# An instruction order from list schedules made forwards and backwards, in a fused attention and two-layer network kernel

## The chip, the cores and the metric

The kernel runs on one core of a Trainium2 chip. The metric is the device time of one execution in microseconds (us); lower is better. Of several runs the median counts.

## The reference

Attention over q, k, v of shape 4 x 8 x 576 x 64 (batch, heads, sequence, head size), in float32, with a mask that lets a block of 64 queries see its own and all earlier blocks of 64 keys. Its output, reshaped to 2304 tokens of 512 numbers, goes through two networks:

```python
x = attention(q, k, v)                               # softmax(q k^T / 8 + block mask) v
h = np.maximum(np.maximum(x @ w1, x @ w2), x @ w3)   # w1, w2, w3: 512 x 768
y = h @ w_out                                        # 768 x 512
h = y @ w_in                                         # 512 x 2048 (moe2)
out = (h * np.cos(h)) @ w_out2                       # 2048 x 512
```

## The kernel before

Matmuls of the networks run in a float32 form of which TensorE takes one pass, so every operand is split into a high and a low part and each product is three matmuls (high x high, high x low, low x high). The weights arrive as 64-bit numbers; `convert` makes a high and a low float32 matrix out of each piece of 128 x 512: two scalings, a shift, an and-or, an add, a copy to the high part and a subtraction for the low part. Three of these (and-or, add, subtraction) and the shift always run on VectorE (DVE); the copies and scalings may go to ScalarE (ACT) or VectorE.

**Attention** is 32 items: a batch, one half of the sequence (320 or 256 queries) and a pair of heads. For each item: the scores S (one PSUM buffer, `S`), the row maximum by a VectorE reduction (`stat`), the exponential by ScalarE into the single buffer `prob`, a division by the row sums, transposes on TensorE (`tb`, copied to `pt`), the product with v (`X`) and the split of the result into `xhi` and `xlo`. The first 8 items use plain float32 matmuls, the others the split form.

**The first network** (`moe1_units`) can start on a half of a batch when its four items are done; its three weight pieces per column tile (`whi`, `wlo`) and the output weights (`vhi`, `vlo`) have to be converted by then. Its results (`y`) go to DRAM. **The second network** (`hstage`, `ostage`) runs in chunks of 512 tokens, the last of 256: for each of 16 column tiles `hstage` does 12 matmuls into `psm`, VectorE and ScalarE form h cos(h) and split it (`gh`, `gl`), and `ostage` adds 12 matmuls into the `po` banks two tiles later. Its weights and inputs lie in four pools: `w_in` tiles 0 to 6 and the inputs of the even chunks in `wb`, the other `w_in` tiles in `wc`, the inputs of the odd chunks in `wk2`.

None of this is issued as it is written. The program records operations in a `Plan`: each has its engine, an estimated cost, the operations that it depends on, and its place in the program (`order`). `run` then does a list schedule: it keeps a clock for each engine, takes the engine that can start next, and gives it, of the operations that are ready at that time, the one that comes first in the program. For operations with several possible engines (`ways`) it picks one by estimated end. Each operation is issued the moment it is scheduled, so that this order is the order in each engine's instruction stream. A buffer of a rotation (`bufs` places under one `tag`) may be used once all operations on the buffer `bufs` generations older are done (`older`); which of the places it gets is left to the pool, which hands them out in the order in which buffers are first used. Because every operation is issued through one line of `caller`, line 209, nearly all rows of the profile carry that line, and groups are told apart by their tiles.

Of the kernel before, what the change touches and what calls it, by code (L numbers as in the profile page):

```python
# [101 lines left out]
class Pool:  # L102
# [1 line left out]
        self.plan, self.kw, self.real, self.open_op, self.bufs, self.tags = plan, kw, None, None, [], {}  # L104

    def tile(self, shape, dt, name, tag=None, bufs=1):
        older = None
        if tag is not None:
            gens = self.tags.setdefault(tag, [])
            older = gens[-bufs] if len(gens) >= bufs else None  # L110
        tag = tag or name
        buf = Buf(self, shape, lambda: self.real.tile(shape, dt, name=name, tag=tag, bufs=bufs),
                  self.kw.get("space") == PSUM, dt, older)
        self.bufs.append(buf)
        self.tags.setdefault(tag, []).append(buf)
        dims, step = [], 1
        for n in reversed(shape[1:]):
            dims.insert(0, (0, n, step))
            step *= n
        return View(buf, dims, (), shape[0])  # L120
# [10 lines left out]
class Plan:  # L131
# [20 lines left out]
    def open(self, *after, **kw):  # L152
        pool = Pool(self, kw)
        o = pool.open_op = self.op("CTL")
        o.deps |= {p.close_op for p in after}

        def run():
            pool.real = self.tc.alloc_tile_pool(**kw)
        o.calls.append(run)
        return pool  # L160
# [114 lines left out]
        return (n * 3.3 + 75 if method == "tensor_tensor" else max(400.0, n * 1.04 + 195)), 45.0, method != "memset"  # L275


    def run(self):
        for o in self.ops:
            if o.engine == "CTL":  # L280
                if hasattr(o, "pool"):
                    for b in o.pool.bufs:
                        o.deps |= set(b.ops)
                continue
            for b in o.bufs:
                o.deps.add(b.pool.open_op)
                if b.older is not None:
                    o.deps |= set(b.older.ops)
            o.deps.discard(o)
        users = {o: [] for o in self.ops}  # L290
        missing = {o: len(o.deps) for o in self.ops}
        for o in self.ops:
            for d in o.deps:
                users[d].append(o)
        free = dict.fromkeys(("PE", "DVE", "ACT", "POOL", "SP"), 0.0)
        ready = {e: [] for e in free}
        waiting = {e: [] for e in free}
        load = dict.fromkeys(free, 0.0)
        end, issued, bus, port = {}, 0, 0.0, 0.0

        def finish(o, start, stop):
            end[o] = (start, stop)
            for fn in o.calls:
                fn()
            for u in users[o]:
                missing[u] -= 1
                if not missing[u]:
                    release(u)

        def release(o):  # L310
            at = 0.0
            for d in o.deps:
                if d.engine == "PE" and o.engine == "PE":
                    at = max(at, end[d][1] - d.late)
                else:
                    at = max(at, end[d][1] + (0.0 if d.engine == "CTL" or o.engine == "CTL" else
                                              self.CROSS if end[d][1] > self.EARLY else 35.0))
            if o.engine == "CTL":
                nonlocal issued
                issued += 1  # L320
                finish(o, at, at)
            else:
                if o.ways:
                    def done(way):
                        e, (cost, late, shared), _ = way
                        start = max(free[e] + load[e], at)
                        if shared:
                            start = max(start, port)
                        return start + cost * self.WEIGHT[e] + late
                    o.engine, (o.cost, o.late, o.port), call = min(o.ways, key=done)  # L330
                    o.calls = [call]
                load[o.engine] += o.cost
                heapq.heappush(waiting[o.engine], (at, o.order, o))

        for o in self.ops:
            if not missing[o] and o not in end and not o.deps:
                release(o)
        while issued < len(self.ops):
            best = None
            for e in free:  # L340
                while waiting[e] and waiting[e][0][0] <= free[e]:
                    at, order, o = heapq.heappop(waiting[e])
                    heapq.heappush(ready[e], (order, at, o))
                if ready[e]:
                    t, pick = free[e], ready[e][0]
                    if pick[2].port and port > t:
                        others = [x for x in ready[e] if not x[2].port]
                        if others:
                            pick = min(others)
                        else:  # L350
                            t = port
                elif waiting[e]:
                    pick = waiting[e][0]
                    t = max(pick[0], port if pick[2].port else 0.0)
                else:
                    continue
                if best is None or t < best[0]:
                    best = (t, e, pick)
            assert best, "the plan has a cycle"
            t, e, pick = best  # L360
            o = pick[2]
            if ready[e]:
                ready[e].remove(pick)
                heapq.heapify(ready[e])
            else:
                heapq.heappop(waiting[e])
            cost = o.cost * (2 if e == "PE" and t < self.COLD else 1)
            free[e] = t + cost
            load[e] -= o.cost
            stop = t + cost + o.late  # L370
            if o.port:
                port = t + cost
            if e == "SP":
                bus = max(bus, t + o.cost) + (o.late - 2000.0)
                stop = bus + 2000.0
            issued += 1
            finish(o, t, stop)
        self.length = max(s[1] for s in end.values())
        self.end = end


def fused_kernel(tc, qk, v2, w1, w2, w3, wout, w_in2, w_out2, out):
# [558 lines left out]
```

## Time and profile before

| | us |
|---|---|
| median of 3 runs | 941.53 |
| lowest and highest run | 940.58 and 943.83 |
| span of the profiled execution, first to last instruction | 944.3 |

Of the profiled execution only the span is given; it lies 2.8 us above the median of the runs and 0.5 us above the highest. The engines in the profile are PE (TensorE's matmuls), PEld (its weight loads), DVE (VectorE), ACT (ScalarE), POOL (GpSimd) and SP (SyncE, which issues the transfers).

### The profile page before, as it was taken

Reading aid. Unit: us, or ns where it says so; the run is one execution under the profiler, and the core shown is the slowest. Engines: PE = TensorE matmul, PEld = TensorE weight load, DVE = VectorE, ACT = ScalarE, POOL = GpSimd, SP = SyncE. Lnnn points to the kernel's source line nnn. Section 1 sums busy time; section 2 is a strip of 40 time slices with the busy share of each in tenths; the row PEclk is TensorE's granted clock in tenths of the full one; section 3 lists DMA queues with packets and bytes.
Section 4 is the critical chain, followed back from the end, with each engine's and each line's share of the span. In section 5 each row is a group of like instructions: output and inputs, shape, how many; then the busy total and the mean of one; then the engine's idle time right before and its main releaser. Section 6 shows DMA issues by size and latency. Waiting matters only on the chain.

```text
span 944.3 us, 14297 instructions
## 1 busy us (share of the span) xinstructions
PE 910.2 (96%) x5388; PEld 806.1 (85%) x5388; DVE 660.9 (70%) x1394; ACT 483.0 (51%) x1088; POOL 0.7 (0%) x7
## 2 busy tenths in 40 slices
PE   5888999999999999999999999999999999999998
PEld 4656989989999999999999988888888888888897
DVE  7878868789888877677676988854555455545454
ACT  5857467677767666656564663332224223322233
POOL 0000000000000000000000000000000000000000
PEclk7989999999999999999999999999999999999999
DMA  6544342433344411212003593120001000100010
GB/s 205 157 153 154 120 140 77 166 111 112 127 143 128 135 51 47 68 41 87 15 1 115 162 386 103 45 66 24 1 1 67 1 1 1 45 0 1 1 45 23
DMA packets 39492, 78.51 MB, mean 83 GB/s; under 512 B 9728, under 2 KB 20992, under 8 KB 39424
## 3 DMA queue, kind: packets, MB, share of 16 engines
q1 hardware_dynamic: 39424, 77.61, 25.4%
q8 instruction: 42, 0.69, 0.3%
q14 instruction: 26, 0.21, 0.1%
HBM read 61.34 MB, written 16.25 MB: 82 GB/s over the span
## 4 chain that ended last, share of the span: by engine, by line
PE 79%; DVE 10%; ACT 7%; issue 2%; DMA 1%; SPq 0%; ACTq 0%
PE psm L209 45%; PE po L209 21%; PE S L209 7%; ACT prob L209 5%; PE tb L209 4%; DVE stat L209 3%; PE X L209 2%; DVE t L209 1%; DVE x L209 1%; DVE vs L209 1%; DVE pt L209 1%; DMA vr<-v 1%; DVE hm L209 1%; ACT pt L209 0%; DMA qk<-qk 0%
## 5 line engine op out<-in xcount | busy, mean ns | idle before, releaser
L209 PE MATMUL psm<-yh,w_in 128*128 128x512 f32 (+1 forms) x640 | 195.8, 372 | 0.0
L209 PE MATMUL psm<-xhi,whi 128*128 128x320 f32 (+1 forms) x576 | 176.6, 307 | 2.9 <-DVE hm L209 1.3
L209 PE MATMUL po<-w_out,gh 128*128 128x512 f32 x576 | 178.8, 392 | 0.0
L209 PE MATMUL psm<-xlo,whi 128*128 128x320 f32 (+1 forms) x576 | 170.9, 297 | 1.2 <-DVE xlo L209 1.2
L209 PE MATMUL psm<-xhi,wlo 128*128 128x320 f32 (+1 forms) x576 | 170.9, 297 | 0.0
L209 ACT ACTIVATE th<-th,halfpi 128x512 f32<-128x512 f32 (+1 forms) x80 | 54.5, 681 | 185.4 <-DVE th L209 185.3
L209 PEld LDWEIGHTS psm<-yh,w_in 128*128 128x128 f32 x640 | 117.2, 188 | 22.8 <-DVE th L209 0.4
L209 PEld LDWEIGHTS po<-w_out,gh 128*128 128x128 f32 x576 | 107.0, 188 | 23.2 <-ACT gh L209 0.4
L209 PE MATMUL psm<-yl,w_in 128*128 128x512 f32 (+1 forms) x320 | 118.8, 371 | 0.0
L209 PEld LDWEIGHTS psm<-xhi,whi 128*128 128x128 f32 x576 | 109.7, 190 | 5.9 <-DVE hm L209 2.8
L209 PE MATMUL po<-w_out,gl 128*128 128x512 f32 x288 | 112.5, 391 | 0.0
L209 PEld LDWEIGHTS psm<-xlo,whi 128*128 128x128 f32 x576 | 109.6, 190 | 1.5 <-DVE xlo L209 1.4
L209 PEld LDWEIGHTS psm<-xhi,wlo 128*128 128x128 f32 x576 | 109.4, 190 | 0.0
L209 DVE TENSOR_SCALAR th<-psm 128x512 int32<-128x512 f32 (+1 forms) x80 | 50.9, 637 | 73.8 <-PE psm L209 70.5
L209 ACT ACTIVATE prob<-S,stat 128x320 f32<-128x320 f32 (+8 forms) x144 | 74.7, 526 | 47.1 <-DVE stat L209 43.3
L209 DVE TENSOR_REDUCE stat<-S 128x1 f32<-128x320 f32 (+8 forms) x144 | 64.5, 485 | 46.6 <-PE S L209 35.5
L209 DVE TENSOR_TENSOR th<-psm,th 128x512 f32<-128x512 f32 (+1 forms) x80 | 51.0, 637 | 53.9 <-ACT th L209 53.9
L209 DVE TENSOR_TENSOR gl<-th,gh 128x512 fp32r<-128x512 f32 (+1 forms) x80 | 50.9, 636 | 37.6 <-ACT gh L209 37.4
L209 ACT CAST gh<-th 128x512 fp32r<-128x512 f32 (+1 forms) x76 | 43.7, 575 | 53.8 <-DVE th L209 53.8
L209 PEld LDWEIGHTS psm<-yl,w_in 128*128 128x128 f32 x320 | 60.2, 188 | 11.5
L209 PE MATMUL tb<-ident,prob 128*128 128x128 f32 x400 | 60.9, 284 | 5.6 <-DVE pt L209 3.2
L209 PEld LDWEIGHTS po<-w_out,gl 128*128 128x128 f32 x288 | 54.1, 188 | 11.7 <-DVE gl L209 0.2
(86 smaller groups left out, 1523.4 us busy)
## 6 DMA issues: line engine op xcount, KB each, us to landing
raw<-w SPq DMA_DIRECT2D x18, 512.0 KB, 3.6
raw<-w_in SPq DMA_DIRECT2D x16, 512.0 KB, 3.8
raw<-w_out SPq DMA_DIRECT2D x16, 512.0 KB, 3.8
vr<-v SPq DMA_DIRECT2D x16, 320.0 KB, 3.4
qk<-qk SPq DMA_DIRECT2D x12, 416.0 KB, 3.5
kept_in<-both SPq DMA_DIRECT2D x9, 512.0 KB, 2.8
w_in<-kept_in SPq DMA_DIRECT2D x9, 512.0 KB, 10.2
out<-osb SPq DMA_DIRECT2D x18, 256.0 KB, 2.0
```

What stands on the lines that cost most here:

```text
L209: return lambda: getattr(real, method)(*[value(a) for a in args], **{k: value(a) for k, a in kw.items()})
```

## The change

`run` no longer issues operations while it schedules. It calls `forward` and `backward` in turn, 8 times. `forward` is the list schedule of before, except that among the ready operations of an engine it takes the one with the lowest `rank`; in the first pass the rank is the place in the program. `backward` makes a list schedule from the end of the program to its start, on the engines that the forward pass chose, and notes for each operation the time at which it starts there, counted from the beginning, with the length of the forward pass as the end. That time is the rank of the next forward pass. Of the 8 forward passes the one with the shortest planned length is issued, in its order and with its choice of engines. Costs, dependencies and the rule that an engine never idles while one of its operations is ready stay as they were.

In `Pool.tile` each place of a rotation becomes a tag of its own with one buffer; generation n of a tag always gets place n modulo `bufs`.

```diff
     def tile(self, shape, dt, name, tag=None, bufs=1):
-        older = None
-        if tag is not None:
-            gens = self.tags.setdefault(tag, [])
-            older = gens[-bufs] if len(gens) >= bufs else None
-        tag = tag or name
-        buf = Buf(self, shape, lambda: self.real.tile(shape, dt, name=name, tag=tag, bufs=bufs),
+        gens = self.tags.setdefault(tag or name, [])
+        older = gens[-bufs] if tag is not None and len(gens) >= bufs else None
+        slot = f"{tag or name}_{len(gens) % bufs}"
+        buf = Buf(self, shape, lambda: self.real.tile(shape, dt, name=name, tag=slot, bufs=1),
                   self.kw.get("space") == PSUM, dt, older)
         self.bufs.append(buf)
-        self.tags.setdefault(tag, []).append(buf)
+        gens.append(buf)
...
+    ENGINES = ("PE", "DVE", "ACT", "POOL", "SP")
+    PASSES = 8
+
+    def after(self, d, o, stop):
+        if d.engine == "PE" and o.engine == "PE":
+            return -d.late
+        if d.engine == "CTL" or o.engine == "CTL":
+            return 0.0
+        return self.CROSS if stop > self.EARLY else 35.0
+
+    def spent(self, o, start):
+        return o.cost * (2 if o.engine == "PE" and start < self.COLD else 1)
+
+    def forward(self, rank):
+
+        missing = {o: len(o.deps) for o in self.ops}
+        free = dict.fromkeys(self.ENGINES, 0.0)
+        ready = {e: [] for e in free}
+        waiting = {e: [] for e in free}
+        load = dict.fromkeys(free, 0.0)
+        end, chosen, bus, port = {}, {}, 0.0, 0.0
+
+        def finish(o, start, stop):
+            end[o] = (start, stop)
+            for u in self.users[o]:
+                missing[u] -= 1
+                if not missing[u]:
+                    release(u)
+
+        def release(o):
+            at = max((end[d][1] + self.after(d, o, end[d][1]) for d in o.deps), default=0.0)
+            at = max(at, 0.0)
+            if o.engine == "CTL":
+                finish(o, at, at)
+                return
...
+            load[o.engine] += o.cost
+            heapq.heappush(waiting[o.engine], (at, rank[o], o.order, o))
+
+        for o in self.ops:
+            if not o.deps:
+                release(o)
...
+                while waiting[e] and waiting[e][0][0] <= free[e]:
+                    at, r, order, o = heapq.heappop(waiting[e])
+                    heapq.heappush(ready[e], (r, order, at, o))
+                if ready[e]:
+                    t, pick = free[e], ready[e][0]
...
+        return end, chosen, max(s[1] for s in end.values())
+
+    def backward(self, end, length):
+
+
+        missing = {o: len(self.users[o]) for o in self.ops}
+        free = dict.fromkeys(self.ENGINES, 0.0)
+        ready = {e: [] for e in free}
+        waiting = {e: [] for e in free}
+        latest = {}
+
+        def finish(o, stop):
+            latest[o] = length - stop
+            for d in o.deps:
+                missing[d] -= 1
+                if not missing[d]:
+                    release(d)
+
+        def release(o):
+            start, stop = end[o]
+            late = stop - start - (0.0 if o.engine == "CTL" else self.spent(o, start))
+            at = max((length - latest[u] + self.after(o, u, stop) + late for u in self.users[o]), default=0.0)
+            if o.engine == "CTL":
+                finish(o, at)
+            else:
+                heapq.heappush(waiting[o.engine], (at, -start, -o.order, o))
+
+        for o in self.ops:
+            if not self.users[o]:
+                release(o)
+        while len(latest) < len(self.ops):
+            best = None
+            for e in free:
+                while waiting[e] and waiting[e][0][0] <= free[e]:
+                    heapq.heappush(ready[e], heapq.heappop(waiting[e])[1:])
+                if ready[e] or waiting[e]:
+                    t, o = (free[e], ready[e][0][2]) if ready[e] else (waiting[e][0][0], waiting[e][0][3])
+                    if best is None or t < best[0]:
+                        best = (t, e, o)
+            t, e, o = best
+            heapq.heappop(ready[e] or waiting[e])
+            free[e] = t + self.spent(o, end[o][0])
+            finish(o, free[e])
+        return latest
+
...
-        users = {o: [] for o in self.ops}
-        missing = {o: len(o.deps) for o in self.ops}
+        self.users = {o: [] for o in self.ops}
         for o in self.ops:
...
-                users[d].append(o)
-        free = dict.fromkeys(("PE", "DVE", "ACT", "POOL", "SP"), 0.0)
-        ready = {e: [] for e in free}
-        waiting = {e: [] for e in free}
-        load = dict.fromkeys(free, 0.0)
-        end, issued, bus, port = {}, 0, 0.0, 0.0
-
...
+                self.users[d].append(o)
+        rank, best = {o: o.order for o in self.ops}, None
+        for _ in range(self.PASSES):
+            end, chosen, length = self.forward(rank)
+            if best is None or length < best[2]:
+                best = end, chosen, length
+            rank = self.backward(end, length)
+        self.end, chosen, self.length = best
+        for o in self.end:
+            if o in chosen:
+                o.engine, (o.cost, o.late, o.port), call = chosen[o]
+                o.calls = [call]
...
-        def release(o):
-            at = 0.0
-            for d in o.deps:
-                if d.engine == "PE" and o.engine == "PE":
-                    at = max(at, end[d][1] - d.late)
-                else:
-                    at = max(at, end[d][1] + (0.0 if d.engine == "CTL" or o.engine == "CTL" else
-                                              self.CROSS if end[d][1] > self.EARLY else 35.0))
...
-                heapq.heappush(waiting[o.engine], (at, o.order, o))
```

What is left out of `forward` (the choice of engine, the shared port, the transfer bus) is as in the old `run`.

## Rows read from the trace of the kernel before

**Rows 1.** the page, busy time of each engine over the whole span
```profile
PE 910.2 (96%) x5388; PEld 806.1 (85%) x5388; DVE 660.9 (70%) x1394; ACT 483.0 (51%) x1088; POOL 0.7 (0%) x7
```

**Rows 2.** six stretches (us): length, each engine's busy time, TensorE's clock, DMA share, GB/s
```profile
0.00:88.50 88.50, 67.64 (x336) 48.06 (x336) 71.57 (x192) 59.96 (x150) 0.74 (x7) 0.90 0.54 167
88.50:213.00 124.50, 119.20 (x857) 114.71 (x858) 101.12 (x234) 80.50 (x201) 0.00 (x0) 0.99 0.38 127
213.00:507.50 294.50, 290.10 (x2087) 279.68 (x2086) 226.35 (x521) 192.27 (x484) 0.00 (x0) 1.00 0.25 78
507.50:555.40 47.90, 47.89 (x346) 45.23 (x346) 40.61 (x83) 29.51 (x55) 0.00 (x0) 1.00 0.66 222
555.40:889.80 334.40, 334.40 (x1455) 273.24 (x1454) 195.43 (x303) 102.29 (x162) 0.00 (x0) 1.00 0.12 38
889.80:944.30 54.50, 50.98 (x313) 45.14 (x311) 25.78 (x66) 18.45 (x39) 0.00 (x0) 0.99 0.08 30
```

**Rows 3.** waits of TensorE, 0 to 120 us, the second longest
```profile
PE S L209 <- ACT prob L209: 4.2, 4, 1.7
```

**Rows 4.** waits of TensorE, 120 to 545 us, the longest
```profile
PE tb L209 <- DVE pt L209: 3.2, 3, 1.9
PE psm L209 <- ACT vhi L209: 1.4, 1, 1.4
```

**Rows 5.** TensorE in order of time: start, length, what [idle before <-releaser]
```profile
6.39 1.85 PE L209 MATMUL S<-qk,qnat 128*128 128x320 f32 x10
15.87 3.68 PE L209 MATMUL S<-qk,qnat 128*128 128x320 f32 x10 [7.63 <-DMA qk<-qk]
29.81 1.09 PE L209 MATMUL S<-qk,qnat 128*128 128x256 f32 x6 [1.99 <-DVE stat L209]
...
65.22 3.37 PE L209 MATMUL S<-qk,qnat 128*128 128x288 f32 x8 [1.70 <-ACT prob L209]
78.34 1.99 PE L209 MATMUL S<-qk,qnat 128*128 128x288 f32 x8 [1.70 <-ACT prob L209]
...
198.44 1.71 PE L209 MATMUL tb<-ident,prob 128*128 128x128 f32 x8 [1.93 <-DVE pt L209]
```

**Rows 6.** all engines in order of time, 6 to 30 us
```profile
9.44 0.43 DVE L209 TENSOR_SCALAR t<-raw 128x512 f32<-128x512 f32 x1 [0.90 <-DMA raw<-w]
11.80 0.75 DVE L209 TENSOR_REDUCE stat<-S 128x1 f32<-128x320 f32 x2
...
15.87 0.50 PEld L209 LDWEIGHTS S<-qk,qnat 128*128 128x128 f32 x2 [7.76 <-ACT prob L209]
27.40 0.69 DVE L209 SCALAR_TENSOR_TENSOR t<-raw,t 128x512 int32<-128x512 int32 x1
29.01 0.74 DVE L209 TENSOR_REDUCE stat<-S 128x1 f32<-128x320 f32 x2
```

**Rows 7.** all engines in order of time, 194 to 200 us
```profile
196.51 1.06 ACT L209 CAST pt<-tb 128x512 fp32r<-128x512 f32 x2
196.52 0.76 DVE L209 TENSOR_REDUCE stat<-S 128x1 f32<-128x576 f32 x1
197.70 1.29 DVE L209 TENSOR_TENSOR pt<-tb,pt 128x512 fp32r<-128x512 f32 x2
```

**Rows 8.** TensorE and its clock from 200 to 205 us
```profile
200.00:205.00 5.00, 5.00 (x28) 4.86 (x28) 3.32 (x7) 3.24 (x8) 0.00 (x0) 0.78 0.42 147
```

**Rows 9.** a conversion's instruction: count | busy us, mean ns of one | idle before
```profile
L209 DVE SCALAR_TENSOR_TENSOR t<-raw,t 128x512 int32<-128x512 int32 x56 | 38.5, 687 | 0.7
```

**Rows 10.** the chain that ended last: start us, us, what
```profile
88.52 28.42 PE psm L209 x192
664.33 2.72 PE psm L209 x12
779.93 2.81 PE psm L209 x12
841.01 2.72 PE psm L209 x12
```

More of the change, by code (lines that the diff above doesn't have):

```diff
@@ new lines, in forward, with done @@
+    def forward(self, rank):
[17 more added lines that the diff above has]
+                return
+            if o.ways:
+                def done(way):
+                    e, (cost, late, shared), _ = way
+                    start = max(free[e] + load[e], at)
+                    if shared:
+                        start = max(start, port)
+                    return start + cost * self.WEIGHT[e] + late
+                chosen[o] = min(o.ways, key=done)
+                o.engine, (o.cost, o.late, o.port), _ = chosen[o]
+            load[o.engine] += o.cost
[3 more added lines that the diff above has]
+                release(o)
+        while len(end) < len(self.ops):
+            best = None
[5 more added lines that the diff above has]
+                    t, pick = free[e], ready[e][0]
+                    if pick[3].port and port > t:
+                        others = [x for x in ready[e] if not x[3].port]
+                        if others:
+                            pick = min(others)
+                        else:
+                            t = port
+                elif waiting[e]:
+                    pick = waiting[e][0]
+                    t = max(pick[0], port if pick[3].port else 0.0)
+                else:
+                    continue
+                if best is None or t < best[0]:
+                    best = (t, e, pick)
+            assert best, "the plan has a cycle"
+            t, e, pick = best
+            o = pick[3]
+            if ready[e]:
+                ready[e].remove(pick)
+                heapq.heapify(ready[e])
+            else:
+                heapq.heappop(waiting[e])
+            free[e] = t + self.spent(o, t)
+            load[e] -= o.cost
+            stop = free[e] + o.late
+            if o.port:
+                port = free[e]
+            if e == "SP":
+                bus = max(bus, t + o.cost) + (o.late - 2000.0)
+                stop = bus + 2000.0
+            finish(o, t, stop)
+        return end, chosen, max(s[1] for s in end.values())
@@ new lines, in backward @@
+    def backward(self, end, length):
[16 more added lines that the diff above has]
+                finish(o, at)
+            else:
+                heapq.heappush(waiting[o.engine], (at, -start, -o.order, o))
[3 more added lines that the diff above has]
+        while len(latest) < len(self.ops):
+            best = None
+            for e in free:
+                while waiting[e] and waiting[e][0][0] <= free[e]:
+                    heapq.heappush(ready[e], heapq.heappop(waiting[e])[1:])
+                if ready[e] or waiting[e]:
+                    t, o = (free[e], ready[e][0][2]) if ready[e] else (waiting[e][0][0], waiting[e][0][3])
+                    if best is None or t < best[0]:
+                        best = (t, e, o)
[4 more added lines that the diff above has]
+        return latest
@@ L301, in finish @@
-        def finish(o, start, stop):
-            end[o] = (start, stop)
+                self.users[d].append(o)
[10 more added lines that the diff above has]
+                o.calls = [call]
@@ L303, in finish @@
             for fn in o.calls:
                 fn()
[L305 to L308, printed above, removed]
-        def release(o):
-            at = 0.0
-            for d in o.deps:
-                if d.engine == "PE" and o.engine == "PE":
-                    at = max(at, end[d][1] - d.late)
-                else:
-                    at = max(at, end[d][1] + (0.0 if d.engine == "CTL" or o.engine == "CTL" else
-                                              self.CROSS if end[d][1] > self.EARLY else 35.0))
[L318 to L332, printed above, removed]
-                heapq.heappush(waiting[o.engine], (at, o.order, o))
@@ L335, in run @@
[L335 to L377, printed above, removed]
@@ L378, in run @@
-        self.length = max(s[1] for s in end.values())
-        self.end = end
 def fused_kernel(tc, qk, v2, w1, w2, w3, wout, w_in2, w_out2, out):
```

## Prediction

> **What bounds the kernel now.** I read the totals of the page first. TensorE is busy for 910.2 of 944.3 us, VectorE for 660.9, ScalarE for 483.0 [rows 1]. The change removes and adds no arithmetic, so only time in which TensorE stands, or works at its lower clock, can be won. The second view therefore splits the span by stage [rows 2]. TensorE stands 88.5 - 67.6 = 20.9 us while the first items of attention run and the weights are converted, 5.3 us up to 213 us, 4.4 us up to 507.5 us, nothing for the next 382 us, and 3.5 us at the end (last copy and last transfer). Together that is 34.1 us, and 26 of them lie in the first quarter. From 507.5 us on there is nothing to order better: TensorE never waits.
>
> The third view is who ends those waits. In the first 120 us the longest is 7.63 us before the second item's scores [rows 5]. Matmuls name a transfer there, but the weight load in front of them names ScalarE's exponentials [rows 6], because there is one score buffer and the first item's exponentials free it. Follow those back: the first scores were done at 6.39 + 1.85 = 8.24 us [rows 5], VectorE began the row maximum only at 11.80 us, and from 9.44 us it converted weights [rows 6]. The same happens before 29.81 us: TensorE stands 1.99 us for a maximum that began at 29.01 us, behind conversions from 27.40 us on [rows 5, 6]. At 198.44 us TensorE stands 1.93 us for the low part of a transposed tile. ScalarE's part began at 196.51 us, and VectorE did a maximum and an addition in between [rows 5, 7]. So a good part of the waits is a choice of order on VectorE, which is what the change rewrites. Others are not: four waits for exponentials, 4.2 us together [rows 3], are a chain of scores, maximum and exponential with one score buffer.
>
> The clock is the second loss. Ten matmuls of one shape took 1.85 us at 6.39 us and 3.68 us at 15.87 us, after the long gap; eight others took 1.99 us at 78.34 us and 3.37 us at 65.22 us [rows 5]. The granted clock, 1.00 in most stretches, is 0.78 from 200 to 205 us, after the gap at 198 us [rows 8]: its mean over the two levels of 1.2 and 2.4 GHz. That stretch alone lost 0.22 x 5 = 1.1 us.
>
> **The change part by part.** *Fixed places.* The old pool may give a generation another place than the one whose release the plan waited for, which can add waits. TensorE's waits from 213 us on are 4.4 us in all [rows 2], so this is worth 0 to 4.4 us. I take 0, because the longest waits after 120 us end in conversions and transposed tiles [rows 4], not in a buffer taken out of turn. No instruction and no transfer is added.
>
> *The new rank.* No instruction is removed; any of the 7,870 on the three compute engines [rows 1] may change places, and transfers on SP with them. What the rank can do is bounded by the rule that stays: an engine that is free in the plan takes what is ready. A conversion that is ready when nothing else is still goes first. Only where both are ready does the tighter one win. So for each wait caused by order the gain lies between nothing and the delay, and I take about half, since no row says how often both were ready.
>
> 1. First item: the maximum was 11.80 - 8.24 = 3.56 us late. 0 to 3.56, taken 1.8. The clock is low afterwards in any case.
> 2. Gap at 29.81 us: of 1.99 us the conversions explain 29.01 - 27.40 = 1.61. 0 to 1.61, taken 0.8.
> 3. The other waits of the first 88.5 us: 20.9 - 7.63 - 1.99 - 4.2 (exponentials) = 7.1, of which about 1.4 is the start before the first matmul can run. 0 to 5.7, taken a third, 1.9, because they are many and short.
> 4. From 120 us on: 3.2 us for low parts and 1.4 us for a converted weight [rows 4]. 0 to 4.6, taken 2.3.
> 5. The low clock after the gap at 198 us: 0 to 1.1, taken 0.5. If its cause goes, it goes.
> 6. The exponentials' waits: 0 to 4.2 and 1.4 of clock (3.37 - 1.99). Taken 0: a chain is no order.
> 7. The other waits up to 507.5 us and the last 3.5 us: taken 0. A new order can just as well open waits here; VectorE is busy 226 of 294 us and TensorE 290 [rows 2].
>
> Sum: 1.8 + 0.8 + 1.9 + 2.3 + 0.5 = 7.3 us. The profiled 944.3 us become 937.0 us. Against the median of 941.53 us, 2.8 us below that span, the same 7.3 us give **934.2 us**. All upper bounds of 1 to 6 together are 3.6 + 1.6 + 5.7 + 4.6 + 1.1 + 5.6 = 22.2 us, or 919 us.
>
> *Where buffers lie.* Places that are tags of their own, used first in another order, move buffers in SBUF. That may not be free. The same twelve matmuls of the second network take 2.72 us in some stretches and 2.81 us in others [rows 10], with TensorE never waiting. The quick ones are two runs of nine column tiles, which begin at 664.33 and 841.01 us; by the loops they read weights from `wc` and inputs from `wk2`, while others mix pools. From 555.4 to 889.8 us, 1455 matmuls took 334.4 us [rows 2], 229.8 ns each, against 226.7 and 234.2 at the two rates: all quick would be 4.6 us less, all slow 6.3 us more. I take 0 for it and keep both ends.
>
> The Trainium skill (SBUF — State Buffer, section on SBUF's two separate sides) says that contention there is structural and that TensorE's and ScalarE's ports never wait for another engine. By it a move of buffers would cost and give nothing, and the sum stays 934.2 us; the two rates in the trace have no explanation in it, so the measurement keeps the two ends.
>
> **The rivals.**
>
> *Larger gain.* If the rank settles nearly all choices for attention, the sum goes towards its bounds: 12 to 22 us, 920 to 930 us. For it: VectorE is busy 72 of the first 88.5 us [rows 2], much of it with conversions, of which most are not needed until the first network begins at 88.5 us. Against it: engines still take what is ready, and real transfers land when they do (VectorE waited 0.90 us for one at 9.44 us, with the maximum queued behind it, rows 6), which a new rank does not know better.
>
> *No change.* The plan gets shorter only where its estimates think it is long, or the first pass stays the shortest and only places change. Then the waits of rows 4 and 5 come back elsewhere: 939 to 944 us. For it: from 213 to 507.5 us the old order already leaves TensorE 98.5% busy.
>
> *Slower: weights too late.* If attention is preferred on VectorE, conversions are what is late next. Behind them wait the first network's matmuls, and behind those, in TensorE's order, scores of the next items. The trace shows how close that is: 192 matmuls run without a gap from 88.52 us [rows 10], and a converted weight was already waited for, 1.4 us [rows 4]. A piece costs VectorE at least three instructions of 0.69 us [rows 9], 2.1 us. Each piece that slips with nothing else ready holds TensorE that long; the forecast gain is gone after 7.3 / 2.1 = 3.5 pieces. Five make 10.5 - 7.3 = 3.2 us more, 944.7 us; eight make 951 us. It decides from the fifth. Against it: TensorE can run scores and transposes meanwhile, and the rank is made from the matmuls that need those weights. Buffers that land at the slow rate could add up to 6.3 us and end on the same side.
>
> **How the numbers follow.** Forecast, 930 to 938.7 us: 0.45. Larger gain, below 930: 0.20, of which 0.06 lies below 921. No change: 0.15. Slower: 0.20, of which 0.14 lies above 946. A measurement of this kernel tells 0.3% (2.8 us) from no change, so faster means below 938.7 and slower above 944.4. Faster 0.65, same 0.15, slower 0.20. The range is 921 to 946 us; the forecast's own, faster cases alone, is 921 to 938.7.
>
> **What would show it.** Right: the stretch up to 88.5 us ends some 4 us earlier at the same work, the second item's scores begin near 14 us, the longest waits for `stat` and `pt` shrink, and the wait before 200 us with its low clock is gone. From attention's end on, TensorE is as full as before and the stage only starts earlier. Wrong: TensorE's busy time per matmul after attention changes (places), new waits for `whi`, `vhi` or `vlo` appear after 88 us (weights late), or waits for `prob`, `pt` and `hm` between 213 and 507 us grow well past 4.4 us, which would mean that the plan's order is right only on its own clock.

## The result, and the profile after

| | before | changed |
|---|---|---|
| median (us) | 941.56 | 933.69 |
| lowest and highest (us) | 940.58, 943.83 | 933.53, 934.62 |
| span of the profiled execution (us) | 944.3 | 931.4 |

Four runs each; the ratio is 0.9914, with a 95% interval of 0.9898 to 0.9930: 0.9% faster, 0.0086 x 941.56 = 8.1 us. The forecast was 934.2 us.

The profiled execution of before was a late one of its kind: 944.3 us of span against a median time of 941.5. The kernel `e1_places_only` below has the old order by construction (one forward pass in program order) and took the old time; its profiled span is 941.5 us. Where two executions are subtracted, I use that one for the old order, and [rows 2] to [rows 8] for what they show of its waits.

The page of the changed kernel, busy time of each engine; [rows 1] has the same line of before.

```profile
PE 904.1 (97%) x5388; PEld 801.9 (86%) x5388; DVE 663.0 (71%) x1402; ACT 478.9 (51%) x1080; POOL 0.7 (0%) x7
```

TensorE has the same 5388 matmuls and VectorE eight instructions more, which ScalarE has fewer. Nothing was removed, so the gain is time in which TensorE stood or ran at its lower clock. Next the stretches of the changed kernel, up to about where the first network's matmuls begin to run without a gap (86 us), through the stretch in which most waits of the old order behind that lay (210 us), to the beginning of the second network's sums (543 us), and the 334 us behind; then 195 to 205 us by itself. The columns are those of [rows 2]: length, busy time of PE, PEld, DVE, ACT and POOL with the number of instructions, TensorE's clock, DMA share, GB/s.

```profile
0.00:86.00 86.00, 67.55 (x345) 47.34 (x346) 71.38 (x196) 60.10 (x150) 0.74 (x7) 0.94 0.56 175
86.00:210.00 124.00, 122.08 (x893) 117.43 (x894) 106.04 (x248) 81.84 (x203) 0.00 (x0) 1.00 0.39 131
210.00:543.00 333.00, 329.49 (x2388) 318.97 (x2387) 264.38 (x592) 216.11 (x527) 0.00 (x0) 1.00 0.29 97
543.30:877.30 334.00, 334.00 (x1454) 272.71 (x1453) 194.93 (x303) 102.11 (x162) 0.00 (x0) 1.00 0.12 40
195.00:205.00 10.00, 10.00 (x66) 9.71 (x65) 9.11 (x22) 6.33 (x15) 0.00 (x0) 1.00 0.34 116
```

The same stretches of the old order with fixed places (`e1_places_only`):

```profile
0.00:86.00 86.00, 66.85 (x336) 47.65 (x336) 71.48 (x192) 59.85 (x150) 0.74 (x7) 0.92 0.55 171
86.00:210.00 124.00, 118.66 (x853) 114.18 (x854) 100.67 (x234) 80.08 (x201) 0.00 (x0) 0.99 0.38 126
210.00:543.00 333.00, 328.59 (x2393) 317.59 (x2392) 260.51 (x591) 213.89 (x526) 0.00 (x0) 1.00 0.28 90
552.40:886.40 334.00, 334.00 (x1454) 272.77 (x1453) 195.04 (x302) 101.89 (x162) 0.00 (x0) 1.00 0.12 39
195.00:200.00 5.00, 4.01 (x17) 3.73 (x18) 4.49 (x10) 3.42 (x9) 0.00 (x0) 0.66 0.50 188
```

Subtract busy time from length. TensorE's idle time went from 19.15 to 18.45 us in the first stretch, from 5.34 to 1.92 in the second and from 4.41 to 3.51 in the third: 0.7 + 3.4 + 0.9 = 5.0 us. The clock gives the rest: 0.92 against 0.94 over 86 us is 1.7 us, and the low stretch after 195 us (0.66 over 5 us, 1.7 us) is gone. Together 8.4 us, where these two spans differ by 10.1 and the ratio gives 8.1 (the profiled execution of e1 took 943.25 us, 1.3 above its median). In the second network both orders keep TensorE full and do 1454 matmuls in the same 334.00 us.

The counts of matmuls say it in another way that doesn't lean on idle times. Up to 543 us the changed kernel has done 345 + 893 + 2388 = 3626 and the old order 336 + 853 + 2393 = 3582, 44 fewer; a matmul takes 334.00 / 1454 = 0.230 us there, and 44 x 0.230 = 10.1 us is the difference of the two spans (941.5 - 931.4). At 86 us the lead is 9 matmuls, at 210 us it is 49, at 543 us 44 (a matmul across the edge of a window is counted on both sides, so these are good to one or two).

A matmul is not worth the same everywhere, so the leads have to be turned into time by kind. These are the matmuls into `psm` up to 210 us, of which all but 32 belong to the first network, first in the changed kernel, then in e1:

```profile
0.00:210.00 210.00, 108.77 (x716) 100.02 (x716) 15.39 (x34) 7.23 (x18) 0.98 0.46 149
0.00:210.00 210.00, 101.81 (x683) 95.44 (x684) 14.51 (x32) 7.26 (x18) 0.96 0.45 144
```

They take 0.15 us each, so the 33 more are some 5 us. With 12 more transposes into `tb` (164 against 152, 0.16 us each) and three more scores the lead at 210 us is some 7 us. At 86 us it is between 1 and 2 us: 13 more matmuls of the first network, four fewer products with v. At 543 us the whole lead is matmuls of the second network, 0.230 us each. So of the 10 us between these two spans some 1.5 are won before 86 us, more than half from there to 210 us, and some 3 behind 210 us, although idle time falls by only 0.9 us there: the rest of those 3 us must lie in time that the profile counts as busy.

Then who ends TensorE's waits in the changed kernel, up to 88 us and from 88 to 220 us (total us, times, longest us):

```profile
PE S L207 <- ACT prob L207: 9.5, 8, 2.0
PE S L207 <- DVE stat L207: 2.3, 1, 2.3
...
PE psm L207 <- DVE vlo L207: 0.6, 1, 0.6
PE psm L207 <- ACT vhi L207: 0.4, 1, 0.4
PE S L207 <- ACT prob L207: 0.4, 1, 0.4
PE tb L207 <- DVE pt L207: 0.3, 1, 0.3
```

And in the old order with fixed places:

```profile
PE S L207 <- ACT prob L207: 10.6, 5, 6.4
...
PE S L207 <- DVE stat L207: 1.6, 1, 1.6
...
PE tb L207 <- DVE pt L207: 2.9, 2, 1.9
PE psm L207 <- ACT vhi L207: 1.4, 1, 1.4
PE psm L207 <- DVE vlo L207: 0.4, 1, 0.4
```

Behind 88 us the waits for `pt` and `vhi` fall from 4.3 to 0.7 us. Ahead of it the one long wait for exponentials (6.4 us) is gone, but eight waits of up to 2.0 us, 9.5 us in all, stand where there were five with 10.6. The timeline of the changed kernel shows how (start, length, instructions, [idle before <-releaser]); the rows of before are [rows 5] and [rows 6].

```profile
4.96 3.65 PE L207 MATMUL S<-qk,qnat 128*128 128x320 f32 x10 [1.53 <-DMA qnat<-qk]
...
8.64 0.75 DVE L207 TENSOR_REDUCE stat<-S 128x1 f32<-128x320 f32 x2 [4.17 <-PE S L207]
...
12.72 1.95 PE L207 MATMUL S<-qk,qnat 128*128 128x320 f32 x10 [1.88 <-ACT prob L207]
...
25.63 2.08 PE L207 MATMUL S<-qk,qnat 128*128 128x320 f32 x4 [2.30 <-DVE stat L207]
...
27.85 3.82 PE L207 MATMUL X<-pt,vr 128*64 128x320 f32 x10
```

The first maximum begins at 8.64 us, 0.03 us after the scores end, instead of 3.56 us late. But the scores, begun earlier, took 3.65 us instead of 1.85: the new order does only a quarter of the kernel's 16 matmuls with `ident`, which no result needs, ahead of them (8 of their 32 rows in the profile), where the old one did all. The second scores start at 12.72 us, 3.15 us earlier than in [rows 5]. Then the wait for a maximum is there again, 2.30 us at 25.63 us, and ten products at 27.85 us run at the lower rate (3.82 us, with a granted clock of 0.50 from 25 to 30 us; ten of that shape took 2.30 us at 30.15 us in the old order).

### The profile page after: what moved, and what is told of

Its sections match the earlier page's. It is cut to its first block, busy times and chain, and to the rows that moved or that the text cites. A ratio compares the mean times of both kernels' runs of the same rounds, so it can differ in the third digit from the quotient of the medians.

```text
span 931.4 us, 14314 instructions
## 1 busy us (share of the span) xinstructions
PE 904.1 (97%) x5388; PEld 801.9 (86%) x5388; DVE 663.0 (71%) x1402; ACT 478.9 (51%) x1080; POOL 0.7 (0%) x7
## 4 chain that ended last, share of the span: by engine, by line
PE 85%; DVE 9%; ACT 3%; issue 1%; DMA 1%; ACTq 0%; DVEq 0%; SPq 0%
PE psm L207 50%; PE po L207 21%; PE S L207 8%; PE tb L207 3%; PE X L207 3%; DVE stat L207 3%; ACT prob L207 3%; DVE t L207 2%; DVE pt L207 1%; DVE x L207 1%; DVE hm L207 1%; DVE wlo L207 0%; DMA qk<-qk 0%; DVE qbd L207 0%; DVE prob L207 0%
## 5 line engine op out<-in xcount | busy, mean ns | idle before, releaser
L207 ACT ACTIVATE prob<-S,stat 128x128 f32<-128x128 f32 (+8 forms) x144 | 74.8, 527 | 54.7 <-DVE stat L207 50.2
```

Source lines behind the costliest of these rows:

```text
L207: return lambda: getattr(real, method)(*[value(a) for a in args], **{k: value(a) for k, a in kw.items()})
```

## The experiments

The theory: the gain is the order; it takes waits away that VectorE's old order made, first the late maxima of the first 88 us, then the low parts and converted weights up to 213 us. Rivals: it comes from the places; from transfers that are issued earlier; from the clock in the first microseconds (the matmuls with `ident`); or from TensorE's own order. All kernels but e22 are timed against the kernel before, whose median was 942.67 us in the first batch (e1 to e5), 943.20 in the second (e6 to e11) and 943.28 in the third.

Four columns count the matmuls that TensorE had done (sums of the windows 0 to 86, 86 to 210 and 210 to 543 us), with the span of the same execution; the last has the length that the kernel's own planner gives its order (program order: 923.8 us; with the buffers of e14 it would be 924.9).

| kernel | by 86 us | by 210 | by 543 | span, us | time, us | ratio, 95% | plan, us |
|---|---|---|---|---|---|---|---|
| changed | 345 | 1238 | 3626 | 931.4 | 933.69 | 0.9914 (0.9898, 0.9930) | 909.0 |
| e1 places only | 336 | 1189 | 3582 | 941.5 | 941.92 | 0.9994 (0.9982, 1.0006) | 923.8 |
| e3 rank only | 355 | 1253 | 3635 | 930.0 | 933.22 | 0.9900 (0.9882, 0.9919) | 909.0 |
| e4 new rank early | 333 | 1216 | 3593 | 939.8 | 942.71 | 1.0003 (0.9991, 1.0015) | 919.4 |
| e5 new rank late | 336 | 1216 | 3611 | 935.3 | 937.06 | 0.9935 (0.9919, 0.9952) | 914.5 |
| e6 `ident` matmuls first | 333 | 1233 | 3624 | 932.3 | 934.32 | 0.9909 (0.9891, 0.9928) | 912.5 |
| e7 loads as before | 347 | 1247 | 3625 | 932.0 | 934.68 | 0.9914 (0.9895, 0.9934) | 911.9 |
| e10 vector, scalar | 339 | 1221 | 3610 | 935.5 | 937.22 | 0.9942 (0.9923, 0.9960) | 916.5 |
| e11 tensor | 353 | 1236 | 3612 | 935.0 | 936.62 | 0.9936 (0.9915, 0.9957) | 916.1 |
| e14 scores by bank | 304 | 1182 | 3582 | 941.4 | 943.32 | 1.0000 (0.9990, 1.0010) | 910.5 |
| e20 two prob, bank | 357 | 1258 | 3630 | 930.9 | 932.70 | 0.9886 (0.9870, 0.9902) | 904.5 |
| e21 the same, one pass | 299 | 1156 | 3549 | 949.8 | 952.24 | 1.0096 (1.0079, 1.0112) | 922.4 |

In each row the lead over e1 at 543 us, times 0.230 us, is the difference of the spans to within 0.9 us (e5: 29 x 0.230 = 6.7 against 6.2), so the count at 543 us tells what each kernel has won. At 86 and 210 us the counts mix kinds and show the place of the gain only roughly.

**Places or order.** e1 keeps the fixed places and takes the first pass; e3 keeps the new order and the old `tile`.

```diff
-    PASSES = 8
+    PASSES = 1      # e1
...
-        slot = f"{tag or name}_{len(gens) % bufs}"
+        ...tag=tag, bufs=bufs   # e3: tile as before the change
```

> One forward pass in program order: the old order, with only the places of the buffers fixed. If the new order makes the gain, as forecast (places were taken at 0), this takes the time of before, 940 to 943 us. If places that were given out of turn had held the old order up, it takes most of the gain, 934 to 936 us.

> The new order with the old allocation of places. If the order makes the gain, 933 to 935 us. If places do, or if the new order uses buffers out of turn so that the pool hands out a place that is still taken, it loses part or all of the gain: 937 us and more, with new waits on buffers.

The places alone give 0.9994, no change; the order alone gives 0.9900, the whole gain. The rival of the places falls.

**Where in time.** A mark is set in the program at the step of item 8. e4 uses the new rank for the operations ahead of it and program order behind; e5 the reverse.

```diff
+        if n == 8:
+            R.cut = len(R.ops)
...
+            rank = {o: rank[o] if o.order < self.cut else 1e7 + o.order for o in self.ops}    # e4
+            rank = {o: rank[o] if o.order >= self.cut else o.order - 1e7 for o in self.ops}   # e5
```

> The new rank for operations up to the eighth item of the program (the plain float32 items, all conversions of the first network and its first units), program order behind them. By the prediction's terms 1 to 3 and part of 4, this half carries 4.5 to 6 of the 7.3 us: 936 to 937 us. If the gain lies in the later items, 940 to 942 us.

> Program order up to the eighth item, the new rank behind it. By the prediction's terms little is left here, 1.5 to 3 us: 939 to 940 us. If the gain lies in the later items, 934 to 937 us.

The stretches of e4, the columns as above:

```profile
0.00:86.00 86.00, 65.11 (x333) 45.98 (x334) 69.69 (x190) 61.58 (x152) 0.74 (x7) 0.92 0.56 172
86.00:210.00 124.00, 121.61 (x883) 116.27 (x881) 103.83 (x243) 79.57 (x199) 0.00 (x0) 1.00 0.38 123
210.00:543.00 333.00, 327.75 (x2377) 315.87 (x2377) 258.70 (x585) 213.94 (x526) 0.00 (x0) 1.00 0.29 93
```

And of e5:

```profile
0.00:86.00 86.00, 67.38 (x336) 48.22 (x336) 71.17 (x192) 59.58 (x149) 0.74 (x7) 0.94 0.55 171
86.00:210.00 124.00, 119.66 (x880) 116.05 (x879) 103.29 (x242) 80.91 (x202) 0.00 (x0) 1.00 0.38 123
210.00:543.00 333.00, 329.09 (x2395) 319.10 (x2394) 263.47 (x590) 217.07 (x530) 0.00 (x0) 1.00 0.30 96
```

The new rank ahead of item 8 alone is worth nothing (1.0003). In the first 86 us e4 stands 86.00 - 65.11 = 20.9 us, more than the old order's 19.15. It leads the old order by 27 matmuls at 210 us, and by 11 at 543: much of the lead is given back behind, where program order rules. (The profiled execution of e4 is its quickest, 941.60 us; its median of 942.71 us has no lead left.) e5 leads by 27 at 210 us, matmuls of the first network and transposes, and by 29 of 0.230 us each at 543 us, and has 6.1 of the changed kernel's 8.1 us. The part of my theory that put most of the gain into the first items falls here.

**Which engine.** In e10 only VectorE and ScalarE follow the new rank and the others program order; in e11 only TensorE does.

```diff
+            rank = {o: rank[o] if o.engine in ("DVE", "ACT") else o.order for o in self.ops}   # e10
+            rank = {o: rank[o] if o.engine == "PE" else o.order for o in self.ops}             # e11
```

> The new rank on VectorE and ScalarE only; TensorE and the loads keep program order among ready operations. If the gain is the order on VectorE, as the prediction has it, it stays: 934 to 937 us. If it is TensorE's own order (which ready matmuls go first), 940 to 943 us.

> The new rank on TensorE only; VectorE, ScalarE and the loads keep program order among ready operations. If the gain is the order on VectorE, little is left: 939 to 943 us. If it is TensorE's own order, 934 to 937 us.

The stretches of e10:

```profile
0.00:86.00 86.00, 65.86 (x339) 47.21 (x340) 73.92 (x200) 57.76 (x146) 0.74 (x7) 0.94 0.57 172
86.00:210.00 124.00, 120.66 (x882) 116.34 (x882) 103.83 (x243) 83.65 (x205) 0.00 (x0) 1.00 0.40 131
210.00:543.00 333.00, 330.24 (x2389) 318.41 (x2389) 257.27 (x582) 215.40 (x530) 0.00 (x0) 1.00 0.29 93
```

And of e11:

```profile
0.00:86.00 86.00, 67.26 (x353) 48.46 (x354) 73.89 (x201) 59.12 (x147) 0.74 (x7) 0.96 0.57 177
86.00:210.00 124.00, 121.14 (x883) 116.41 (x882) 104.44 (x243) 81.36 (x201) 0.00 (x0) 1.00 0.38 121
210.00:543.00 333.00, 328.45 (x2376) 316.69 (x2376) 261.19 (x589) 217.47 (x529) 0.00 (x0) 1.00 0.30 97
```

Either alone gives some two thirds: 0.0058 x 943.2 = 5.5 us and 0.0064 x 943.2 = 6.0 us. Their sum, 11.5 us, is more than the 8.1 of both together, so they remove partly the same waits. From 86 to 210 us the idle time of 5.34 us becomes 3.3 in e10 and 2.9 in e11. A wait for a low part ends earlier if VectorE does it first, and it isn't seen if TensorE is given other matmuls meanwhile. "A choice of order on VectorE", as I had it, is half of the story.

**Transfers and the matmuls with `ident`.** e7 lets SP issue its transfers in program order; e6 puts the 16 matmuls with `ident` first again.

```diff
+            rank = {o: o.order if o.engine == "SP" else rank[o] for o in self.ops}   # e7
...
+            rank = {o: -1e7 if o.first else rank[o] for o in self.ops}               # e6
...
-        R.tensor.matmul(warm[:, 0:P], ident, ident, start=True, stop=True)
+        R.tensor.matmul(warm[:, 0:P], ident, ident, start=True, stop=True).first = True
```

> The changed kernel with its loads and stores in program order among those that are ready. If issuing the first queries ahead of the first weights (first scores 1.4 us earlier) is part of the gain, 935 to 937 us; if not, 933 to 935 us.

> The changed kernel, but the 16 idle matmuls at the start, of which the new order puts only 8 before the first scores, are all issued first again. The first ten score matmuls take 1.85 us instead of 3.65. If that low clock costs at the end, 931.5 to 933 us; if the wait for the exponentials covers it, the time of the changed kernel, 933 to 935 us.

Both keep the gain (0.9914 and 0.9909), so the transfers' order is no part of it. e6's timeline of TensorE:

```profile
7.23 1.92 PE L207 MATMUL S<-qk,qnat 128*128 128x320 f32 x10 [0.56 <-DMA qnat<-qk]
17.47 3.68 PE L207 MATMUL S<-qk,qnat 128*128 128x320 f32 x10 [8.31 <-ACT prob L207]
```

The first scores are quick again, but they begin 2.3 us later, and the long gap is back. e6 is 12 matmuls behind the changed kernel at 86 us, 5 at 210, 2 at 543: most of what the first items lose is made up before 210 us. So a loss of this size in the first items hardly reaches the time here; the larger one of e14 below does.

**More freedom for the plan.** If waits for `prob` are what is left in the first 88 us (9.5 us), smaller releases should help. e14 makes the score buffer one lasting tile, so that the next scores may enter a bank that is free instead of waiting for the generation before. e20 adds a second `prob` buffer, with a buffer each taken from three rotations to make room; e21 is e20 in program order.

```diff
+    score = ps_x.tile([P, 2, 512], F32, "S")      # e14, e20, e21
-            s = ps_x.tile([P, 2, 512], F32, "S", tag="S", bufs=1)
+            s = score
...
-    prob = at.tile([P, 17 * P], F32, "prob")
+    probs = [at.tile([P, n * P], F32, f"prob{i}") for i, n in enumerate((17, 16))]   # e20, e21
+    def place(it, b):
+        return probs[it.n % 2 if b else 0]
...
-    PASSES = 8
+    PASSES = 1                                    # e21
```

(In e20 and e21 the rotation `t` goes from 4 to 3 buffers, `hh` and `hl` from 7 to 6.)

> The changed kernel with one score tile for all items in place of a new generation for each, so that each of its two banks is free again when its own exponentials are done. In the first 88 us the changed kernel waits longest for scores that stand behind exponentials, 9.5 us. If the score buffer makes that wait, 929 to 932 us; if the wait is set elsewhere (the single probability buffer, or VectorE), 932.5 to 935 us.

> As before, and with two probability buffers in turn (paid for with one place less in three rotations: t 3, hh 6, hl 6). If the two single buffers together make the waits of the first 88 us, 928 to 931 us; if VectorE is what is late there, 932.5 to 935 us.

> The same buffers with program order among ready operations (one forward pass). If the single buffers became the limit only through the new order, 940 to 943 us, the time of before; if they held the old order up as much, 935 to 938 us.

e14 loses the whole gain against the kernel before, which neither case of its expectation had: its plan is 910.5 us, nearly that of the changed kernel. Its first stretch, and below it the waits up to 88 us:

```profile
0.00:86.00 86.00, 64.33 (x304) 45.29 (x304) 63.44 (x176) 56.56 (x143) 0.74 (x7) 0.88 0.52 161
```

```profile
PE S L207 <- ACT prob L207: 10.5, 8, 3.5
PE S L207 <- DVE stat L207: 3.6, 3, 2.4
PE S L207 <- DMA qnat<-qk: 2.5, 1, 2.5
```

It is 41 matmuls behind the changed kernel at 86 us and never makes them up (56 at 210, 44 at 543). Up to 86 us the idle time is 3.2 us longer than the changed kernel's, and the clock, 0.88 against 0.94 over 86 us, another 5.2 us: 8.4 of the 10.0 us by which the spans differ. The plan takes TensorE at half rate up to 30 us (`COLD`) and at full rate behind; it doesn't know that the clock falls again after a gap. That this is why its length misled here is argued, not shown: no run gave it a better model of the clock. Nor was e14 run in program order, so how much its new order still wins with one score tile is not known.

With two `prob` buffers the bank-wise scores are no loss: 932.70 us. Its ratio of 0.9886 and the changed kernel's 0.9914 come from different batches and their intervals overlap, so e20 is not shown to be better. The same buffers in program order take 952.24 us, 1.0096, outside both cases of the expectation. The stretch up to 86 us of e20:

```profile
0.00:86.00 86.00, 69.30 (x357) 50.22 (x358) 72.45 (x192) 64.95 (x161) 0.74 (x7) 0.90 0.56 178
```

and its waits for exponentials up to 88 us:

```profile
PE S L207 <- ACT prob L207: 10.3, 7, 3.9
```

The stretch of e21:

```profile
0.00:86.00 86.00, 65.12 (x299) 45.31 (x300) 66.39 (x179) 52.50 (x133) 0.74 (x7) 0.84 0.49 153
```

58 matmuls lie between the two at 86 us. So with these buffers the order is worth more, 19.5 us between e21 and e20 against 8 here, because program order does worse, not because the best order does much better. What in program order makes e21 so slow stays open: the score tile, the second `prob` buffer and the three shorter rotations came together.

**Where weights lie.** e22 puts an eighth `w_in` tile into the pool `wb` (7 of 16 before, the rest in `wc`), with `t` at 3 buffers to make room. It was run once, 937.47 us, and serves for its profile alone.

```diff
-    NA = 7
+    NA = 8
...
-                if fc == NFC - 2:
-                    conv_in(NFC - 1, wc)
```

> The changed kernel with 8 instead of 7 tiles of w_in in the pool on the other side (and three places instead of four for t). If the place of the weights sets the two rates of the second network's matmuls (2.72 and 2.81 us for twelve), the quick stretches of the second and fourth chunk shrink from nine tiles to eight; if they depend on something else (transfers, VectorE), nine tiles stay.

The chain that ended last in the changed kernel, with twelve matmuls of the second network to a row (start us, us, what):

```profile
646.17 2.81 PE psm L207 x12
...
651.71 2.72 PE psm L207 x12
...
695.23 2.72 PE psm L207 x12
...
700.67 2.78 PE psm L207 x12
```

And of e22:

```profile
655.65 2.81 PE psm L207 x12
...
661.18 2.72 PE psm L207 x12
...
699.26 2.72 PE psm L207 x12
...
704.71 2.78 PE psm L207 x12
```

The quick run has nine tiles in the changed kernel (651.71 to 695.23 us, every 5.44 us) and eight in e22 (661.18 to 699.26). The second quick run, in the fourth chunk, has nine and eight as well. Moving one weight tile to the other pool took one tile out of it. The rate goes with the pools of weights and inputs, as the prediction read it; why it does, these runs don't show. It had no part in the result, since the pools of the change are those of before. The Trainium skill (SBUF — State Buffer, section on SBUF's two separate sides) says that TensorE's ports never wait for another engine; the equal 334.00 us of both orders agree with that, though no run here sets another engine against it. For the two rates, 2.72 and 2.81 us, the section gives no reason, and there the measurement decides.

## Why the prediction was right, point by point

The time (934.2 forecast, 933.69 measured) and the mechanism, order and not places, were right. The split of the sum was not: too much ahead of 88 us, too little behind, and the two errors cancel. That the number came within 0.5 us is luck.

- *Places, 0 us.* Right: e1 0.9994. *Transfers on SP* are no part of it either (e7).
- *Terms 1 to 3, the first 88.5 us, 4.5 us.* Too large, and this is the step that failed. The late maximum went as foreseen (3.56 us late, now 0.03), and the second scores came at 12.72 us (forecast near 14). But idle time fell by 0.7 us only, and the clock's rows give 1.7, without the slow first scores (3.65 us against 1.85); in work done the lead at 86 us is between 1 and 2 us. Term 2's wait is there as before (2.30 us against 1.99). I had said that the exponentials' waits are a chain and had put them at 0; what I missed, as I read the rows now, is that shortening other waits puts TensorE sooner before the same chain. Eight waits of up to 2.0 us took the place of a 6.4 us gap and four short ones. Alone the early order is worth nothing (e4).
- *Term 4, low parts and weights, 2.3 of at most 4.6.* Too small: the waits for `pt` and `vhi` fall from 4.3 to 0.7 us between 88 and 220 us, and idle time by 3.4. Taking half for want of a row was the error; here TensorE had other matmuls ready, so nearly all could go.
- *Term 5, the low clock, 0.5 of 1.1.* Too small: it is gone with its gap. From 195 to 205 us the clock is 1.00 and TensorE full; in the old order it was 0.66 over 5 us, 1.7 us. The row of [rows 8] held only a part of the low stretch: from 195 to 200 us the kernel before has 0.88, another 0.6 us.
- *Term 7, the waits up to the second network, 0 us.* Too small: 0.9 us of idle time is won behind 210 us, and in work done some 3 us. With terms 4 and 5 this is where the sum fell short.
- *VectorE's choice of order.* Half right: it gives two thirds alone, and so does TensorE's order alone (e10, e11).
- *The rivals.* The first network begins earlier than the 88.5 us taken there: of its matmuls 24 are done by 86 us in the old order and 37 in the changed one (56 and 69 into `psm`, less the 32 rows with `ident`). "Weights too late" did not come: `vhi` and `vlo` cost 1.0 us after 88 us, less than the old order's 1.8, and no `whi` is among the longest waits. "Larger gain", below 930 us, did not come, and a second `prob` buffer (e20) did not bring it: the waits for `prob` stay, 10.3 us in seven. "No change" holds for the early half alone.

Left open: what in e14's order brings the clock down, and whether a plan that knew of the clock would avoid it; and 10.1 - 8.4 = 1.7 us between the two spans that neither idle time nor the clock's rows hold. By the counts of kinds this difference arises behind 210 us; what slows TensorE there in the old order is not known.

## What to carry to other kernels

Value a wait by what its engine runs into next: in a chain with one score buffer a removed wait came back at the next link, while waits that stood alone among work that was ready went nearly whole. Count the matmuls done by a fixed time in both traces, kind by kind, and weigh each kind by its time; the lead and where it arises say where the gain is, even where idle times and clocks are hard to add up. A count of all kinds together misleads: 49 at 210 us and 44 at 543 us are some 7 and 10 us. And rank orders of a planner on the chip: plans of 909.0 and 910.5 us ran at 933.69 and 943.32.

## What the runs showed of the hardware

- The clock's row has a blind spot at the start. In the changed kernel the trace's record of the clock begins 11.0 us after the first instruction (5.2 us in e1), and the row from 5 to 10 us says 1.00 (2.4 GHz), while the ten score matmuls in it took 3.65 us, against 1.95 for ten of the same shape at 12.72 us and 1.92 for the same ten in e6, where all `ident` matmuls ran first:

```profile
5.00:10.00 5.00, 5.00 (x18) 4.43 (x18) 1.28 (x5) 1.97 (x5) 0.00 (x0) 1.00 0.94 299
```

- Twelve matmuls of one shape take 2.72 us or 2.77 to 2.81 us (up to 3.3% more) by the pools in which their weights and inputs lie, with TensorE never waiting; moving one tile to another pool moved the border (e22).
- One order does not always get the same clock: e1 and the kernel before, alike in order, had 0.92 and 0.90 up to 86 and 88.5 us [rows 2], and their spans differ by 2.8 us.
